# Retention and a Strassen-like MoE on one core: loads, GpSimd's share, w2's operands and the last additions put in another order

## The chip, the cores and the metric

The kernel runs on one core of a Trainium2 chip. The core has a matrix engine (TensorE, PE in the profile; its weight loads are PEld), three engines for elementwise work (VectorE is DVE, ScalarE is ACT, GpSimd is POOL) and a queue engine (SyncE, SP) that here issues nearly all DMAs. Each engine works through its own instructions in order and waits for others by semaphores, so an instruction that waits holds up all that stand behind it on the same engine. The metric is the device time of one execution in microseconds; a time is the median of several runs.

## The reference

Two stages follow each other. The first is a retention (a linear attention with decay) over 4 batches, 8 heads, 768 positions and 64 values per head:

```python
for t in range(S):
    state = gamma * state + k[t] (outer) v[t]
    y[t] = scale * q[t] @ state
```

Its output, seen as x of 3072 tokens with 512 values, goes through four experts, every token through all of them, weighted by normalised probabilities p:

```python
for e in range(4):
    h = np.maximum(x @ w1[e], 0.0)            # 512 -> 1024
    out += p[:, e:e + 1] * (h @ w2[e])        # 1024 -> 512
```

Inputs and outputs are float32.

## The kernel before, in words

**Precision.** A float32 product is made of three matmuls of the faster float32r kind: each operand is split into a high part (a copy by ACT, called hi, L237, L278, L287, L446) and a low part (source minus high part, on DVE or POOL, called lo, L241, L283, L291, L451), and hi·hi, hi·lo and lo·hi are added up in PSUM.

**Retention** works in chunks of 128 positions, six per batch. For chunk ci: scale_v multiplies v by the decay inside the chunk (POOL), scores multiplies keys with queries (PE) and masks the result (DVE, L143, tile sp), values multiplies the masked scores with v and the queries with the old state (PE, L181 and L187) and scales the result into xraw (DVE, L196); state makes the chunk's own k·v (PE, L154), added to the old state (DVE, L160), which decay has multiplied before (POOL, L166). values(ci - 1) also issues the matmuls of state(ci).

**The MoE** is cut into rounds: 16 per batch (NRND), each with 256 of the hidden units of one expert, so 64 rounds n in all. In each round x @ w1 is done as a 2x2 block product with 7 instead of 8 multiplications (p1, steps k = 0 to 6 in the order SEQ; i names the product, `p1(n, i)` has six matmuls of 384 columns). It needs sums of blocks of x (combine_x: t1, t2, t4 and one in place) and of w1 (combine_w1), and the products are put together by DVE additions in PSUM (L424) and ACT copies (L418). PSUM has two banks for the running product x, one for y, one for z, two for outputs. The first addition of a round's first result is called c11.

**Batch 0 and the others differ.** In batch 0, while w1 and w2 of a round come from memory for the first time, the hidden values get ReLU (ACT, L438) and low part (DVE, L439), and `p2(n - 1, tile)` multiplies 128 tokens of the round before with w2 (six matmuls of 512 columns); DVE adds the result, weighted with pm, to acc (L549). Beside it, weights(n, k), called once per step, splits w1 of round n + 1 and w2 of round n and writes all split operands to memory (save_w1, save_w2): w2's plain parts (hi2 and lo2 with wt2) and its combined ones (combine_w2, in place, then hi2 and lo2 with wc2). Later batches fetch them from there (fetch_w1 four steps ahead, fetch_w2). In these batches (n >= 16) the second product also has 7 multiplications and runs over pairs of rounds q: unit(q, s) with s = 0 to 13 is product UNITS[s] for one half d of the output. Its operands come from gated: ReLU times gate on DVE (L458), differences on POOL (L460), op_hi and op_lo. A unit's result is added to sums in SBUF (L582 for sum with sum, L424 for PSUM with sum), and the last pair of a batch leads to finish, which joins the sums and stores them. The units of the very last pair run after all rounds, alone: the tail.

**Order.** The whole program is written out by hand (`tc.manual_schedule()`); the framework places only semaphores and buffers. Within a step the order is: fetches, pass_step (runs what was put in the list soon with a delay in steps), p1, unit or p2, low parts of x of the next batch (in round 15 of a batch), weights, and a part of the next batch's retention (att_steps). A buffer is given again when its last reader is done: raw w1 has two, raw w2 one, plain w2 operands two, combined ones one, fetched w1 five. Batch 0's chunk loads borrow buffers of weights not yet in use.

Of the kernel before, what the change touches and what calls it, by code (L numbers as in the profile page):

```python
# [22 lines left out]
XPOOL = (1, 3)  # L23
WARM = (384, 384, 384, 384)
# [19 lines left out]
LAST_UNITS = tuple((i, d) for i in (1, 3, 5, 7, 6, 4, 2) for d in range(2))  # L44
# [7 lines left out]
def retention_moe(ctx: ExitStack, tc: tile.TileContext, qk, kv, w1, w2, probs, probt, cmask, cqs, cks, cys, out, out_t):  # L52
# [67 lines left out]
    def load_kv(ci, pool=None, tag=None, eng=None):  # L120
        if ci < NCH:
            t = (pool or in_p).tile([128, 2, H, D], F32, tag=tag or "kv", name="kv", bufs=None if pool else 2)
            (eng or nc.sync).dma_start(out=t, in_=kv[ci])
            raw_kv[ci] = t
# [186 lines left out]
    def units(q):  # L311
        return LAST_UNITS if q == NP * B - 1 else UNITS

# [8 lines left out]
    def fetch_w2(g):  # L322
        q, k = divmod(g, 7)
        if q < NP * B:
            i = units(q)[2 * k][0]
# [3 lines left out]
    def first_x(c, part):  # L329
        o = slice(C * c, C * c + C)  # L330
        combine_x(0, c, nc.vector, nc.gpsimd, part)
        for i in (7, 3, 4) if part else (5, 6):
            x_hi(0, i, o)
            x_lo(0, i, o)

    def weights(n, k):

        m = n + 1
        if n == 0:
            if k == 0:  # L340
# [107 lines left out]
    def op_lo(n, i):  # L448
        hi, lo, t = op[n, i]
        eng = nc.gpsimd if i in LO_POOL else nc.vector  # L450
        eng.tensor_tensor(out=lo, in0=t, in1=hi.bitcast(F32), op=ALU.subtract)  # L451

    def gated(n, key, src):

        f, j = key
        t = npool["b"].tile([128, HB], F32, tag="b", name="b")
# [4 lines left out]
        if key in ((0, 0), (1, 1)):  # L461
            i = 1 if key == (0, 0) else 3
            soon.append((0, lambda: op_hi(n, i, t)))
            soon.append((1, lambda: op_lo(n, i)))
        elif key == (0, 1):
            b11, b22, b12 = hb[n, (0, 0)], hb[n, (1, 1)], t

            soon.append((1, lambda: (sub(b11, b12, b11), sub(b12, b22, b12), sub(b22, b22, b11))))
            soon.append((2, lambda: op_hi(n, 5, b11)))
            soon.append((2, lambda: op_lo(n, 5)))  # L470
            soon.append((3, lambda: (op_hi(n, 7, b12), op_hi(n, 6, b22))))
            soon.append((3, lambda: (op_lo(n, 7), op_lo(n, 6))))
        else:
            b22 = hb[n, (1, 1)]
            soon.append((1, lambda: op_hi(n, 2, t)))
            soon.append((2, lambda: op_lo(n, 2)))
            soon.append((3, lambda: sub(t, t, b22)))
            soon.append((4, lambda: op_hi(n, 4, t)))
            soon.append((5, lambda: op_lo(n, 4)))
# [77 lines left out]
    def unit(q, k):  # L557
        i, d = units(q)[k]
# [18 lines left out]
    def finish(b, i, d):  # L577
# [255 lines left out]
```

## Time and profile before

| | |
|---|---|
| time, median of 3 runs | 1083.79 us (1083.56 to 1084.08) |
| the profiled execution | 1080.76 us |
| its span, first to last instruction | 1078.9 us |
| busy: PE, DVE, POOL, ACT | 1048.2, 731.2, 673.0, 378.7 us |
| granted TensorE clock, mean | 0.993 |
| moved by DMA | 293.70 MB, 272 GB/s over the span |
| the chain that ended last, by engine | PE 85%, DVE 8%, issue 3%, DMA 2% |

Rows of the profile's groups give engine, line, operation, the tiles written and read, shapes and count, then busy time in us and the mean duration of one in ns, then idle time of the engine before them and what ended it. Rows of a timeline give the start in us, the duration in us (of several merged instructions, from the first's start to the last's end), the engine and line, and in brackets the idle time before with the instruction that ended it. In the table by stage, each engine's busy time is followed by its number of instructions in parentheses. A matmul's duration is its latency; consecutive ones overlap.

### The profile page before, as it was taken

To read this page: it belongs to the slowest core of one execution; us is meant where nothing else is said; L and a number is where in the kernel's file an instruction comes from. 1 tells how busy PE (TensorE), PEld (TensorE's weight loads), DVE (VectorE), ACT (ScalarE), POOL (GpSimd) and SP (SyncE) were. 2 spreads that over 40 slices of the span, in tenths; PEclk is the share of its full clock that TensorE was granted. 3 is DMA by queue.
4 is the path that set the end of the run, shared out by engine and by line. 5 is a ranking of instruction groups with operands and counts; after the bars stand their busy time and mean duration, and the time that the engine had idled before them with its cause. 6 is when DMAs were issued, how large, how long until landed. Compare 5 with 4: busy or idle time off the path is not lost.

```text
span 1078.9 us, 18574 instructions
## 1 busy us (share of the span) xinstructions
PE 1048.2 (97%) x6696; PEld 991.3 (92%) x6696; DVE 731.2 (68%) x1221; ACT 378.7 (35%) x737; POOL 673.0 (62%) x638
## 2 busy tenths in 40 slices
PE   7789999999999999999999999999999999999997
PEld 5578888888888999999999999999999999999996
DVE  5957666666676476676679566677678746667667
ACT  2343433444443423222253433322234443333331
POOL 3577676767626556556479655656568865555566
PEclk9899999999999999999999999999999999999999
DMA  8479999899988788878788987888788988888875
GB/s 327 147 255 330 348 303 310 296 349 309 310 293 304 259 272 269 273 249 262 263 256 263 315 278 234 278 261 262 233 254 266 288 271 251 262 259 255 265 235 176
DMA packets 154603, 293.70 MB, mean 272 GB/s; under 512 B 12688, under 2 KB 77328, under 8 KB 154512
## 3 DMA queue, kind: packets, MB, share of 16 engines
q1 hardware_dynamic: 153792, 291.66, 83.0%
q8 instruction: 53, 0.87, 0.3%
q10 hardware_dynamic: 720, 0.86, 0.2%
q14 instruction: 38, 0.31, 0.1%
HBM read 223.22 MB, written 69.26 MB: 271 GB/s over the span
## 4 chain that ended last, share of the span: by engine, by line
PE 85%; DVE 8%; issue 3%; DMA 2%; POOL 1%; ACT 1%; ACTq 0%; SPq 0%; POOLq 0%; DVEq 0%
PE ps_u L567 31%; PE ps_x L506 23%; PE ps_z L506 11%; PE ps_o L541 10%; PE ps_y L506 5%; PE ps_s L140 2%; PE ps_v L187 2%; DVE xl L241 1%; DVE sum L582 1%; DMA w2r<-in_w 1%; PE ps_v L181 1%; DVE ol L451 1%; DMA w1r<-in_w 1%; DVE sum L424 1%; DMA ks<-in_cks 1%
## 5 line engine op out<-in xcount | busy, mean ns | idle before, releaser
L567 PE MATMUL ps_u<-oh,v 128*128 128x384 f32 x1344 | 395.2, 335 | 5.7 <-DVE sum L424 5.4
L460 POOL TENSOR_TENSOR b<-b 128x384 f32<-128x384 f32 x192 | 204.6, 1066 | 175.2 <-DVE b L458 145.4
L451 POOL TENSOR_TENSOR ol<-b,oh 128x384 fp32r<-128x384 f32 x192 | 211.2, 1112 | 81.8 <-ACT oh L446 44.6
L567 PEld LDWEIGHTS ps_u<-oh,v 128*128 128x128 f32 x1344 | 247.7, 188 | 8.7 <-DVE sum L424 7.3
L424 DVE TENSOR_TENSOR sum<-ps_u,sum 128x384 f32<-128x384 f32 x294 | 161.6, 550 | 134.2 <-PE ps_u L567 134.2
L446 ACT ACTIVATE oh<-b 128x384 fp32r<-128x384 f32 x336 | 163.5, 520 | 201.1 <-POOL b L460 109.0
L506 PE MATMUL ps_x<-xh,v 128*128 128x384 f32 x768 | 227.3, 337 | 0.7 <-ACT u L418 0.7
L567 PE MATMUL ps_u<-ol,v 128*128 128x384 f32 x672 | 224.9, 335 | 0.0
L418 ACT ACTIVATE u<-ps_x 128x384 f32<-128x384 f32 x128 | 62.7, 490 | 246.0 <-PE ps_x L506 245.9
L506 PEld LDWEIGHTS ps_x<-xh,v 128*128 128x128 f32 x768 | 141.4, 188 | 3.0 <-ACT u L418 1.0
L451 DVE TENSOR_TENSOR ol<-b,oh 128x384 fp32r<-128x384 f32 x144 | 130.3, 905 | 15.3 <-ACT oh L446 15.3
L506 PE MATMUL ps_x<-xl,v 128*128 128x384 f32 x384 | 128.4, 334 | 0.0
L567 PEld LDWEIGHTS ps_u<-ol,v 128*128 128x128 f32 x672 | 126.3, 188 | 0.0
L506 PE MATMUL ps_z<-xh,v 128*128 128x384 f32 x384 | 113.9, 337 | 2.2 <-DVE c2l L291 1.8
L549 DVE SCALAR_TENSOR_TENSOR acc<-ps_o,pm,acc 128x512 f32<-128x512 f32 x90 | 67.0, 744 | 51.9 <-PE ps_o L541 51.9
L541 PE MATMUL ps_o<-w2h,hh 128*128 128x512 f32 x192 | 75.5, 393 | 0.3 <-DVE acc L549 0.2
L541 PE MATMUL ps_o<-w2h,hl 128*128 128x512 f32 x192 | 75.8, 395 | 0.0
L541 PE MATMUL ps_o<-w2l,hh 128*128 128x512 f32 x192 | 75.8, 395 | 0.0
L506 PEld LDWEIGHTS ps_z<-xh,v 128*128 128x128 f32 x384 | 70.7, 188 | 3.7 <-DVE c2l L291 2.1
L506 PEld LDWEIGHTS ps_x<-xl,v 128*128 128x128 f32 x384 | 72.1, 188 | 0.1
L506 PE MATMUL ps_z<-xl,v 128*128 128x384 f32 x192 | 64.2, 334 | 0.0
L424 DVE TENSOR_TENSOR ps_y<-ps_y,u 128x384 f32<-128x384 f32 x64 | 36.0, 563 | 32.0 <-PE ps_y L506 32.0
(109 smaller groups left out, 1627.9 us busy)
## 6 DMA issues: line engine op xcount, KB each, us to landing
v<-k SPq DMA_DIRECT2D x336, 256.0 KB, 3.9
v<-k SPq DMA_DIRECT2D x168, 512.0 KB, 4.5
k<-w1h SPq DMA_DIRECT2D x16, 896.0 KB, 6.3
k<-w1l SPq DMA_DIRECT2D x16, 896.0 KB, 8.1
qk<-in_qk SPq DMA_DIRECT2D x24, 512.0 KB, 5.6
kv<-in_kv SPq DMA_DIRECT2D x23, 512.0 KB, 5.7
w1r<-in_w SPq DMA_DIRECT2D x16, 512.0 KB, 7.9
w2r<-in_w SPq DMA_DIRECT2D x16, 512.0 KB, 4.2
```

The source lines that it names most:

```text
L140: nc.tensor.matmul(ps[r][:, p, :], lhsT=a[rows, 1, p, :], rhs=a[rows, 0, p, :], start=True, stop=True)
L181: nc.tensor.matmul(ps[r][64 * k:64 * k + 64, half, :], lhsT=yst[(c - 1) % 2][rows, p, :], rhs=raw_qk[ci][rows, 0, p, :], start=(half == 0) ...
L187: nc.tensor.matmul(ps[r][64 * k:64 * k + 64, half, :], lhsT=v[:, 1, h, :], rhs=sp[:, h, :], start=(c == 0 and half == 0), stop=True, skip_ ...
L418: nc.scalar.activation(out=t, in_=ps, func=ACTF.Copy)
L424: nc.vector.tensor_tensor(out=o, in0=ps, in1=u, op=ALU.add)
L446: nc.scalar.activation(out=hi, in_=t, func=ACTF.Copy)
L451: eng.tensor_tensor(out=lo, in0=t, in1=hi.bitcast(F32), op=ALU.subtract)
L460: sub = lambda o, a, b: nc.gpsimd.tensor_tensor(out=o, in0=a, in1=b, op=ALU.subtract)
L506: nc.tensor.matmul(ps, lhsT=lhsT[:, cs], rhs=rhs[:, kt, :], start=(fresh and m == 0), stop=(m == 5), skip_group_check=True,)
L541: nc.tensor.matmul(ps, lhsT=a[:, ts], rhs=b[:, fs, :], start=(m == 0), stop=(m == 5))
L549: nc.vector.scalar_tensor_tensor(out=acc[nt], in0=ps, scalar=sc, in1=acc[nt], op0=ALU.mult, op1=ALU.add)
L567: nc.tensor.matmul(ps, lhsT=w[:, r, l, ds], rhs=o, start=(m == 0), stop=(m == 5))
```

## The change: what it does

Five things are put in another order or given to another engine.

1. *Loads and batch 0's retention.* mask and ks are loaded ahead of the first kv on ACT's queue; on SP's queue all twelve chunk loads and w1(0) come ahead of w2(0), w1(1) and the probabilities, and chunks 3 and 4 of kv go to the buffers of w2's combined operands. scale_v(ci + 1) is issued ahead of decay(ci + 1). Combining w1(0), its low parts, and the low parts of x parts 1 and 3 go from DVE to POOL; w2(0)'s low part and the probabilities' normalisation (first_gates) move into round 0; x parts 3, 4 and 7 are split whole and not chunk by chunk.
2. *Round 0.* w1(1)'s high parts move to steps 4 and 5, its low parts are both POOL's.
3. *w2's operands, rounds 1 to 15.* The plain parts of w2(n) are made in steps 4 and 5 (before: 1 and 2) and saved in step 6 with combine_w2 behind; the combined parts follow in steps 0 to 2 of the next round. load_w2(n) is issued in step 1 of round n (before: step 5 of round n - 1), save_w1 one step earlier.
4. *The change from batch 0 to batch 1.* The first four fetches of w1 are issued at the start of round 14; in round 15 POOL makes the low parts of five of the seven x parts (before: two); in round 16 the delays of gated are doubled. In all later rounds the operands 6 and 7 are made ahead of 5.
5. *The tail.* The last pair uses the same order of units as all others; 3 and 5 get the sums of others earlier, and unit 5 is added from PSUM to both 3 and 5; the halves of finish change engines, and the last low part of operand 5 goes to DVE.

```diff
+XPOOL0 = (0, 2, 4, 5, 6)
-LAST_UNITS = tuple((i, d) for i in (1, 3, 5, 7, 6, 4, 2) for d in range(2))
...
-    def first_x(c, part):
-        o = slice(C * c, C * c + C)
+    def first_part(c, part):
         combine_x(0, c, nc.vector, nc.gpsimd, part)
-        for i in (7, 3, 4) if part else (5, 6):
-            x_hi(0, i, o)
-            x_lo(0, i, o)
+        if part == 0:
+            o = slice(C * c, C * c + C)
+            for i in (5, 6):
+                x_hi(0, i, o)
+            for i in (5, 6):
+                x_lo(0, i, o)
     def weights(n, k):
         m = n + 1
         if n == 0:
             if k == 0:
-                first_x(2, 0)
-                first_x(1, 1)
-                first_x(2, 1)
+                x_hi(0, 3)
+                for c in range(3):
+                    first_part(c, 1)
+                x_hi(0, 7)
+                x_lo(0, 7)
+                x_hi(0, 4)
+                x_lo(0, 3, eng=nc.gpsimd)
+                x_lo(0, 4)
                 combine_w1(1, nc.gpsimd)
+                first_gates()
             elif k == 3:
                 kept.pop("c11")()
+            elif k == 4:
                 w1_hi(1, 0)
-                w1_lo(1, 0, nc.vector)
-                load_w1(2)
+                w1_lo(1, 0, nc.gpsimd)
+                lo2(0, wt2, nc.vector)
+            elif k == 5:
                 w1_hi(1, 1)
                 w1_lo(1, 1, nc.gpsimd)
-            elif k == 4:
-                save_w2(0, wt2, 0)
-                combine_w2(0, nc.gpsimd)
-            elif k == 5:
-                hi2(0, wc2, "c2")
                 save_w1(0)
             elif k == 6:
-                lo2(0, wc2, nc.vector)
-                load_w2(1)
-                save_w1(1)
+                combine_w2(0, nc.gpsimd)
+                save_w2(0, wt2, 0)
             return
         if k == 0:
-            save_w2(n - 1, wc2, 4)
+            if n == 1:
+                save_w1(1)
+            hi2(n - 1, wc2, "c2")
             if m < NRND:
                 load_w1(m + 1)
                 combine_w1(m, nc.gpsimd)
                 w1_hi(m, 0)
         elif k == 1:
-            hi2(n, wt2, "w2")
+            lo2(n - 1, wc2, nc.vector)
+            load_w2(n)
             if m < NRND:
                 w1_lo(m, 0, nc.gpsimd)
         elif k == 2:
-            lo2(n, wt2, nc.vector)
+            save_w2(n - 1, wc2, 4)
             if n == 2:
                 gates()
-        elif k == 3:
-            save_w2(n, wt2, 0)
-            combine_w2(n, nc.gpsimd)
-            if m < NRND:
-                w1_hi(m, 1)
+        elif k == 3 and m < NRND:
+            w1_hi(m, 1)
         elif k == 4:
-            hi2(n, wc2, "c2")
-        elif k == 5:
+            hi2(n, wt2, "w2")
             if m < NRND:
                 w1_lo(m, 1, nc.gpsimd)
-            lo2(n, wc2, nc.vector)
-            load_w2(n + 1)
-        elif k == 6 and m < NRND:
-            save_w1(m)
+        elif k == 5:
+            lo2(n, wt2, nc.vector)
+            if m < NRND:
+                save_w1(m)
+        elif k == 6:
+            combine_w2(n, nc.gpsimd)
+            save_w2(n, wt2, 0)
...
     def op_lo(n, i):
-        eng = nc.gpsimd if i in LO_POOL else nc.vector
+        eng = nc.gpsimd if i in LO_POOL and not (i == 5 and n == NRND * B - 1) else nc.vector
...
     def gated(n, key, src):
+        slow = 2 if n == NRND else 1
+        later = lambda w, what: soon.append((w * slow, what))
...
-            soon.append((2, lambda: op_hi(n, 5, b11)))
-            soon.append((2, lambda: op_lo(n, 5)))
-            soon.append((3, lambda: (op_hi(n, 7, b12), op_hi(n, 6, b22))))
-            soon.append((3, lambda: (op_lo(n, 7), op_lo(n, 6))))
+            later(2, lambda: (op_hi(n, 6, b22), op_lo(n, 6)))
+            later(2, lambda: (op_hi(n, 7, b12), op_lo(n, 7)))
+            later(3, lambda: (op_hi(n, 5, b11), op_lo(n, 5)))
...
     def unit(q, k):
+        elif q == NP * B - 1 and i == 5:
+            for o in (3, 5):
+                add(ps, psum[b, o, d], psum[b, o, d])
         else:
             add(ps, psum[b, i, d], psum[b, i, d])
...
     def finish(b, i, d):
         if b == B - 1:
-            e = (pool, dve)[d]
+            e = (dve, pool)[d]
             if i == 1:
                 sums(1, e, 2, 1)
-            elif i == 5:
-                sums(1, e, 3, 5)
             elif i == 6:
                 sums(0, e, 6, 1)
+                sums(1, e, 3, 6)
+                sums(1, e, 3, 5)
+            elif i == 7:
                 sums(0, e, 7, 6)
-                sums(0, e, 3, 6)
+                sums(0, e, 5, 7)
+                sums(1, e, 4, 7)
+            elif i == 5:
                 store(0, 3, 0, 1)
-                sums(0, e, 5, 7)
                 store(0, 5, 1, 1)
             elif i == 4:
-                sums(0, e, 4, 7)
                 store(0, 4, 1, 0)
...
+        nc.scalar.dma_start(out=mask, in_=cmask)
+        nc.scalar.dma_start(out=ks, in_=cks)
         load_qk(0)
         load_kv(0, eng=nc.scalar)
...
+        load_w1(0)
         load_qk(3, w_p, "w1l")
-        load_w1(0)
+        load_kv(3, v_p, "c2h", 1)
+        load_qk(4)
+        load_kv(4, v_p, "c2l", 1)
+        load_qk(5, v_p, "w2h")
+        load_kv(5, v_p, "w2l")
+        load_w2(0)
+        load_w1(1)
         nc.sync.dma_start(out=pr, in_=probs)
         nc.sync.dma_start(out=gr, in_=probt)
...
+        scale_v(0)
         for ci in range(NCHB):
             old = ci > 0
-            scale_v(ci)
             scores(ci)
             if ci == 5:
-                first_x(0, 1)
+                first_part(0, 0)
...
             if ci + 1 < NCHB:
+                scale_v(ci + 1)
                 decay(ci + 1)
             if ci == 1:
                 w1_hi(0, 0)
-                combine_w1(0, nc.vector)
-                w1_lo(0, 0, nc.vector)
+                combine_w1(0, nc.gpsimd)
             elif ci == 2:
                 w1_hi(0, 1)
-                w1_lo(0, 1, nc.vector)
...
+                w1_lo(0, 0, nc.gpsimd)
             elif ci == 3:
-                hi2(0, wt2, "w2")
-                lo2(0, wt2, nc.vector)
                 for i in (1, 2):
                     x_hi(0, i)
-                    x_lo(0, i)
             elif ci == 4:
-                first_x(0, 0)
+                w1_lo(0, 1, nc.gpsimd)
+                x_lo(0, 1, eng=nc.gpsimd)
+                x_lo(0, 2)
+                hi2(0, wt2, "w2")
+                load_w1(2)
...
-            elif ci == 5:
-                first_x(1, 0)
         start[0] = False
+        first_part(1, 0)
         values(ci, False)
+        first_part(2, 0)
...
-                fetch_w1(t + 4)
+                if t == 7 * (NRND - 2):
+                    for x in range(4):
+                        fetch_w1(7 * NRND + x)
+                if t >= 7 * NRND:
+                    fetch_w1(t + 4)
...
-                    e = nc.gpsimd if k in XPOOL else nc.vector
+                    e = nc.gpsimd if k in (XPOOL if g else XPOOL0) else nc.vector
...
-                if n == NRND and k == 0:
+                elif n == NRND and k == 0:
+                    hi2(n - 1, wc2, "c2")
+                elif n == NRND and k == 1:
+                    lo2(n - 1, wc2, nc.vector)
                     save_w2(n - 1, wc2, 4)
```

More of the change, by code (lines that the diff above doesn't have):

```diff
@@ L118, in load_qk, with load_kv @@
             raw_qk[ci] = t
-    def load_kv(ci, pool=None, tag=None, eng=None):
+    def load_kv(ci, pool=None, tag=None, bufs=None, eng=None):
         if ci < NCH:
-            t = (pool or in_p).tile([128, 2, H, D], F32, tag=tag or "kv", name="kv", bufs=None if pool else 2)
+            t = (pool or in_p).tile([128, 2, H, D], F32, tag=tag or "kv", name="kv", bufs=bufs if pool else 2)
             (eng or nc.sync).dma_start(out=t, in_=kv[ci])
@@ L309, in retention_moe @@
     wp1, wp2 = {}, {}
-    def units(q):
-        return LAST_UNITS if q == NP * B - 1 else UNITS
     def fetch_w1(g):
@@ L324, in fetch_w2 @@
         if q < NP * B:
-            i = units(q)[2 * k][0]
+            i = UNITS[2 * k][0]
             wp2[q, i] = npool["v2"].tile([128, 2, 2, 256], F32R, tag="v2", name="v2")
             nc.sync.dma_start(out=wp2[q, i].bitcast(F32), in_=kept2[q % NP][:, A2_AT[i]])
-    def first_x(c, part):
-        o = slice(C * c, C * c + C)
+    def first_part(c, part):
         combine_x(0, c, nc.vector, nc.gpsimd, part)
-        for i in (7, 3, 4) if part else (5, 6):
-            x_hi(0, i, o)
-            x_lo(0, i, o)
+        if part == 0:
[4 more added lines that the diff above has]
+                x_lo(0, i, o)
     def weights(n, k):
@@ L462, in gated @@
             i = 1 if key == (0, 0) else 3
-            soon.append((0, lambda: op_hi(n, i, t)))
-            soon.append((1, lambda: op_lo(n, i)))
+            later(0, lambda: op_hi(n, i, t))
+            later(1, lambda: op_lo(n, i))
         elif key == (0, 1):
             b11, b22, b12 = hb[n, (0, 0)], hb[n, (1, 1)], t
-            soon.append((1, lambda: (sub(b11, b12, b11), sub(b12, b22, b12), sub(b22, b22, b11))))
-            soon.append((2, lambda: op_hi(n, 5, b11)))
-            soon.append((2, lambda: op_lo(n, 5)))
-            soon.append((3, lambda: (op_hi(n, 7, b12), op_hi(n, 6, b22))))
-            soon.append((3, lambda: (op_lo(n, 7), op_lo(n, 6))))
+            later(1, lambda: (sub(b11, b12, b11), sub(b12, b22, b12), sub(b22, b22, b11)))
+            later(2, lambda: (op_hi(n, 6, b22), op_lo(n, 6)))
+            later(2, lambda: (op_hi(n, 7, b12), op_lo(n, 7)))
+            later(3, lambda: (op_hi(n, 5, b11), op_lo(n, 5)))
         else:
             b22 = hb[n, (1, 1)]
[L475 to L479, printed above, removed]
+            later(1, lambda: op_hi(n, 2, t))
+            later(2, lambda: op_lo(n, 2))
+            later(3, lambda: sub(t, t, b22))
+            later(4, lambda: op_hi(n, 4, t))
+            later(5, lambda: op_lo(n, 4))
     def pass_step():
@@ L557, in unit @@
     def unit(q, k):
-        i, d = units(q)[k]
+        i, d = UNITS[k]
         b, qb = divmod(q, NP)
@@ L654, in retention_moe @@
         nc.vector.memset(warm, 0.0)
+        nc.scalar.dma_start(out=mask, in_=cmask)
+        nc.scalar.dma_start(out=ks, in_=cks)
         load_qk(0)
         load_kv(0, eng=nc.scalar)
-        nc.scalar.dma_start(out=ks, in_=cks)
-        nc.scalar.dma_start(out=mask, in_=cmask)
+        nc.scalar.dma_start(out=ys, in_=cys)
         nc.scalar.dma_start(out=qs, in_=cqs)
@@ L661, in retention_moe @@
         load_kv(1)
-        nc.scalar.dma_start(out=ys, in_=cys)
         load_qk(2, v_p, "w2l")
         load_kv(2, w_p, "w1h")
+        load_w1(0)
         load_qk(3, w_p, "w1l")
-        load_w1(0)
+        load_kv(3, v_p, "c2h", 1)
[5 more added lines that the diff above has]
+        load_w1(1)
         nc.sync.dma_start(out=pr, in_=probs)
         nc.sync.dma_start(out=gr, in_=probt)
-        load_w2(0)
-        load_qk(4)
-        load_kv(3)
-        load_qk(5, v_p, "w2h")
-        load_kv(5, v_p, "w2l")
-        load_kv(4)
-        load_w1(1)
         wps = ps_z.tile([128, 512], F32, tag="z", name="ps_w")
```

9 lines of the change are left out of this document (5 added, 4 removed).

## The prediction

> **What bounds the kernel now.** I read the page's engine shares first, then a table of busy time by stage, then what TensorE (PE) waited for, and last the timelines of the stages in which it waited.
>
> ```profile
> PE 1048.2 (97%) x6696; PEld 991.3 (92%) x6696; DVE 731.2 (68%) x1221; ACT 378.7 (35%) x737; POOL 673.0 (62%) x638
> ```
> ```profile
> 0.00:25.00 25.00, 17.70 (x224) 13.09 (x226) 14.11 (x29) 4.38 (x5) 7.12 (x11) 0.95 0.94 352
> 25.00:50.00 25.00, 18.71 (x176) 15.34 (x174) 24.12 (x40) 10.07 (x23) 13.76 (x14) 0.85 0.49 159
> 50.00:75.00 25.00, 20.19 (x108) 17.20 (x109) 14.32 (x23) 9.58 (x16) 19.42 (x18) 1.00 0.62 200
> 75.00:100.00 25.00, 24.93 (x137) 21.88 (x136) 16.58 (x27) 11.01 (x18) 15.71 (x16) 1.00 0.94 317
> ...
> 300.00:350.00 50.00, 46.88 (x251) 42.00 (x250) 33.19 (x51) 20.22 (x40) 23.66 (x22) 1.00 0.93 318
> ...
> 1060.00:1079.00 19.00, 12.22 (x60) 10.75 (x60) 12.14 (x18) 0.52 (x1) 11.11 (x10) 0.86 0.54 184
> ```
>
> PE is busy for 1048.2 of 1078.9 us. The columns of the table are the stretch, its length, then busy time of PE, its weight loads, VectorE (DVE), ScalarE (ACT) and GpSimd (POOL), the granted clock, the DMA share and GB/s. The 30.7 us that are missing lie in few places: 18.4 in the first 75 us (7.3, 6.3 and 4.8), 3.1 at 300 to 350, 6.8 after 1060. From 75 us on PE has 24.93 of 25. Only these three places can give anything, and the long middle can only lose. In the first, DVE is the limit: 24.12 of 25 at 25 to 50 us, with PE at a clock of 0.85 besides.
>
> ```profile
> 6.08 1.16 PE L140 MATMUL ps_s<-qk 64*128 64x128 f32 x16
> ...
> 17.00 1.16 PE L140 MATMUL ps_s<-qk 64*128 64x128 f32 x16
> ...
> 23.12 1.12 PE L154 MATMUL ps_v<-kv 128*64 128x64 f32 x16 [2.72 <-POOL kv L128]
> 24.17 2.08 PE L140 MATMUL ps_s<-qk 64*128 64x128 f32 x16
> ...
> 37.97 0.69 PE L506 MATMUL ps_x<-xh,w1h 128*128 128x384 f32 x1
> ...
> 54.70 0.39 PE L541 MATMUL ps_o<-w2h,hh 128*128 128x512 f32 x1
> ...
> 57.76 0.45 PE L506 MATMUL ps_x<-xh,w1h 128*128 128x384 f32 x1 [1.51 <-ACT u L418]
> ...
> 65.02 0.44 PE L506 MATMUL ps_x<-xh,w1h 128*128 128x384 f32 x1 [2.11 <-ACT u L418]
> ```
>
> Retention of batch 0 ends at 37.97, where round 0's first matmul starts. One wait for scaled values (2.72) is followed by scores that take 2.08 instead of 1.16: PE at half clock. The first token matmul (p2) comes at 54.70; after it two waits for ACT remain, 1.51 and 2.11.
>
> **The change, part by part. 1: retention of batch 0.**
>
> ```profile
> L241 DVE TENSOR_TENSOR xl<-t,xh 128x256 fp32r<-128x256 f32 x9 | 7.3, 840 | 0.0
> L143 DVE TENSOR_TENSOR sp<-ps_s,mask 128x512 f32<-128x512 f32 x8 | 5.1, 677 | 0.0
> L196 DVE TENSOR_TENSOR xr<-ps_v,qs 128x256 f32<-128x256 f32 x11 | 4.1, 411 | 0.0
> ...
> L241 DVE TENSOR_TENSOR xl<-xr,xh 128x768 fp32r<-128x768 f32 x2 | 3.1, 1578 | 0.0
> ...
> L160 DVE TENSOR_TENSOR yst<-ps_v,yst 128x256 f32<-128x256 f32 x4 | 1.6, 411 | 0.0
> L213 DVE TENSOR_TENSOR t<-xr,t 128x256 f32<-128x256 f32 x3 | 1.6, 524 | 0.1
> L213 DVE TENSOR_TENSOR t<-xr 128x256 f32<-128x256 f32 x3 | 1.2, 407 | 0.0
> ...
> L291 DVE TENSOR_TENSOR w2l<-w2r,w2h 128x1024 fp32r<-128x1024 f32 x1 | 1.2, 1212 | 0.0
> ```
> ```profile
> 50.34 2.39 POOL L283 TENSOR_TENSOR w1l<-s,w1h 128x1024 fp32r<-128x1024 f32 x1 [3.71 <-ACT w1h L278]
> 52.68 0.74 POOL L296 TENSOR_TENSOR w2r<-w2r 128x256 f32<-128x256 f32 x1
> ...
> 59.81 1.84 POOL L283 TENSOR_TENSOR w1l<-w1r,w1h 128x768 fp32r<-128x768 f32 x1
> ```
>
> These are the groups of DVE between 14 and 50 us, and POOL's prices. w1's combination (4 operations), both its low parts and two x low parts of round 0 go to POOL: 4 x 0.74 + 2.39 + 3 x 1.84 = 10.9 us there. w2's low part (1.2) and the gates go behind; x's parts 3, 4 and 7 become whole operations (128x768), nine of 128x256 become two on DVE and one on POOL. By 14.4 us DVE has done chunk 1's state, which I leave where it is. From there to the first addition of round 0 (c11) it keeps masks 5.1; values 10 x 0.37 = 3.7; states 3 x 0.4 = 1.2; combinations of x 1.6 + 1.2 = 2.8; six low parts of a chunk 6 x 0.84 = 5.0; three whole ones 3 x 1.58 = 4.7; the gates about 1.6 (an estimate: four small operations at the 0.4 of the nearest rows). That is 24.1, so c11 at 38.5, and with about 1 us in which DVE waits for PE, 39.5.
>
> PE allows it: scores came at 6.08 and, three chunks on, at 17.00, so 3.64 a chunk with the waits for scaled values in it. With scale_v ahead of decay on POOL, and mask and ks ahead of the first kv, six chunks end at 28 us at the latest. The loads allow it too: 352 GB/s over the first 25 us brings the twelve chunk loads and w1 (6.8 MB) in by some 20 us. Their order costs nothing while a pair (1 MB, 3.0 us) lands in less than a chunk takes; without that cover each late pair costs its delay once. load_w2(0), load_w1(1) and the probabilities move behind the chunks on SP's queue; POOL needs w1(1) and DVE the probabilities only past 30 us.
>
> ```profile
> 47.51 0.55 DVE L424 TENSOR_TENSOR ps_y<-ps_y,u 128x384 f32<-128x384 f32 x1
> ```
>
> c11 stood at 47.51, so 8.0 earlier. Both ends: without any contention (0.42 for 128x256, 0.95 for 128x768) DVE keeps some 18 to 19 us, but part 7's combinations on POOL then hold c11 at about 36.5; if every two-input operation of DVE and every one of POOL exclude each other, the list after 22 us (DVE 7.9, POOL 13.5) ends at 43.4.
>
> The Trainium skill speaks against this part (SBUF — State Buffer, Who interferes with whom): a DVE instruction with two SBUF inputs and a GpSimd instruction that reads SBUF exclude each other for the whole instruction. By that rule this step would gain 4.1 and not 8.0. The groups above show the effect (840 ns for what takes 410 alone), but the tail's rows below show less than full exclusion.
>
> **2: rounds 0 and 1.** After c11 everything is a chain, because w1_hi(1,·) now stand behind the ReLUs of steps 4 and 5 on ACT, lo2(0) stands ahead of the addition of step 5 on DVE, and both w1_lo(1,·) are POOL's: c11 and its parts 1.7, the next addition with ReLU and low part 1.5, lo2 1.2 (+0.6 against POOL), addition and ReLU 1.0, w1_hi about 1.0, w1_lo 2.39, the rest of p1(1,5) 0.9, dispatch 0.5: 10.8. The first p2 comes at 50.3 instead of 54.70: of the 8.0, 4.4 survive.
>
> ```profile
> 63.53 1.06 ACT L287 ACTIVATE w2h<-w2r 128x1024 fp32r<-128x1024 f32 x1 [4.71 <-DMA w2r<-in_w]
> ```
> ```profile
> 75.98 1.39 PE ps_o L541 x6
> 77.37 1.04 PE ps_x L506 x6
> ```
>
> Then the waits of 1.51 and 2.11 go. The second arose because ACT stood 4.71 behind w2(1)'s load; hi2(1) now comes at step 4. The first came from hi2(0,c2) behind POOL's combine_w2. That wait stays on ACT, half a round later: with w1_lo(1,1) done at T, combine_w2(0) ends at T + 3.0, hi2 T + 4.1, w1_hi(2,0) T + 4.9, two copies T + 5.9; PE asks for the second at T + 7.2 (two p1 at 1.04, three p2 at 1.39 and the 0.9). Hidden by 1.3 us. So 4.4 + 3.6 = **8.0** for parts 1 and 2, between 4 and 11.
>
> **3: rounds 1 to 15.** Same operations, same bytes, other places.
>
> ```profile
> w1r<-in_w SPq DMA_DIRECT2D x16, 512.0 KB, 7.9
> w2r<-in_w SPq DMA_DIRECT2D x16, 512.0 KB, 4.2
> ```
>
> load_w2(n) moves from step 5 of the round before to step 1, past save_w1 (2 DMAs), save_w2 of the plain half (2) and load_w1. So it meets the backlog that w1's load meets now: 7.9 us to landing, not 4.2. A round is 7 p1 and 6 p2, 15.6 us, and about 16.2 with scores and values of the next batch. Issued when lo2 of the combined half is done (1.04 + 1.04 + 1.2 = 3.3 us into the round), it lands at 11.2; hi2 stands at step 4 (9.4), behind it on ACT are the ReLUs of steps 5 and 6 and the first copy of the next round; p2 asks for w2's parts and these ReLUs at 18.3. hi2 and lo2 take 2.3, so 4.8 us are spare: nothing. POOL's three combinations and low parts per round keep their sum. I take **0**; a landing later than 12.7 us after issue would cost its excess in each of 15 rounds.
>
> **4: the change of batch (300 to 350).**
>
> ```profile
> 309.30 1.66 SPq L320 DMA_DIRECT2D v<-k  x1
> ```
> ```profile
> 316.26 0.41 PE L506 MATMUL ps_z<-xh,v 128*128 128x384 f32 x1 [1.78 <-DVE c2l L291]
> ```
>
> PE waits 1.78 for its second operand of round 16. The wait is put down to c2l, which that matmul does not read; its operand's fetch was issued at 309.30 behind saves. I take the fetch for the cause. Either way it goes: the first four fetches come two rounds earlier, and c2l a step later with x's low parts moved from DVE (three of 0.95) to POOL, which has no w1 work in round 15. hi2(15,c2) can hold ACT for some 3.4 us of round 16, under the six p2 of steps 1 to 3. I take **-2.0** with 0.2 of a smaller wait; ends 0 and -2.7.
>
> **5: the tail.**
>
> ```profile
> L582 POOL TENSOR_TENSOR sum<-sum 128x384 f32<-128x384 f32 x7 | 8.2, 1189 | 1.6 <-DVE sum L424 1.5
> ...
> L582 DVE TENSOR_TENSOR sum<-sum 128x384 f32<-128x384 f32 x7 | 7.2, 1047 | 0.1
> ```
> ```profile
> 1057.40 0.53 ACT L446 ACTIVATE oh<-b 128x384 fp32r<-128x384 f32 x1 [0.56 <-POOL b L460]
> ```
> ```profile
> 1072.34 0.44 PE L567 MATMUL ps_u<-oh,v 128*128 128x384 f32 x1 [3.14 <-DVE sum L424]
> ```
> ```profile
> 1058.81 0.56 DVE L424 TENSOR_TENSOR sum<-ps_u,sum 128x384 f32<-128x384 f32 x1
> ...
> 1075.47 0.56 DVE L424 TENSOR_TENSOR sum<-ps_u,sum 128x384 f32<-128x384 f32 x1 [1.14 <-PE ps_u L567]
> ```
>
> The 3.14 us wait goes: four sums in a row on DVE held the accumulators. But the count of sums stays 7 on each engine, two PSUM additions (0.56 each) and lo5 come to DVE, and 6 and 7 now come before 5. hi6 waits for POOL's third difference until 1057.40, and hi7, hi2, hi5 stand behind it at some 0.5 each. DVE holds at lo5, ahead of the addition of unit 3,0, until hi5 (1059.3) and POOL's lo6 and lo7 (1060.1, at 1.1 each, an estimate between 0.74 for 256 elements and 1.84 for 768). lo2 and one sum follow, so that addition runs at about 1061.5 and not 1058.8, and PE, with two accumulators, starts unit 6,0 2.1 us late. After it, sums at 1.05 beside POOL hold PE by 1 to 1.6 us at units 5 and 4, and the last addition ends at 1076.7 against 1076.0; with sums at 0.56 PE sets the pace and it ends at 1073.6. Ends +0.7 and -2.4; I take **-0.8**.
>
> **The sum**: -8.0 - 2.0 - 0.8 = -10.8. The profiled run took 1080.76, so 1070.0; the median of the runs is 3.03 above it, so 1083.79 - 10.8 = **1073.0**. Best ends: -11 - 2.7 - 2.4 = -16.1, 1067.7. Worst: -4 + 0 + 0.7 = -3.3, 1080.5.
>
> **Rivals.** *Contention eats the start*: c11 at 43.4, the upper end of part 1, gives 4.1 less in parts 1 and 2; with the rest as forecast -6.9, 1076.9. For it: POOL's load between 22 and 43 us doubles. Against it: seven pairs of sums took 8.2 and 7.2 us, about 1.2 a pair, where exclusion would need 0.56 and some 1.0 (POOL's estimate above) one after the other. It is what the section of the Trainium skill named in part 1 would make of this change. *Everything free*: DVE and the tail at their uncontended prices, -16, 1067.8. *Nothing gained*: a chunk's load or the chain of part 2 takes the place of DVE and the first p2 stays at 54.7; the two ACT waits (3.6) are moved and not removed; only parts 4 and 5 are left: -2.8, 1081.0. Against it: the groups show 10 us of work leaving DVE. *Slower*: w2 lands late in every round, because save_w1, save_w2 and load_w1 are ahead of it on SP's queue at a DMA share of 0.94. It decides beyond 12.7 us from issue to landing; one us past it costs 15, so -10.8 + 15 = +4, 1088. Against it: w1's load, in the same place now, takes 7.9.
>
> **Chances**: forecast 0.50, contention 0.20, free 0.12, nothing 0.08, slower 0.10. A difference of 0.2% (2.2 us) is about what can be told from none. Faster takes the first three and the edge of the fourth, 0.83; same the rest of the fourth, whose time lies at that mark, 0.07; slower 0.10. The range holds the first three with the bounds above: 1067 to 1080.
>
> **What would show it.** Part 1: the first matmul of round 0 near 27 to 29 us, scores at 1.16 throughout, c11 at 36 to 43. Part 2: first p2 at about 50, and no ACT wait of over 1 us behind it. Part 3: PE at 24.9 of 25 from 75 to 300 us, w2's landing under 12 us. Part 4: no wait of 1.8 us at the second operand of round 16. Part 5: no wait of 3 us, a wait of about 2 at unit 6,0. It is wrong if PE has gaps that recur every 16 us, or if the first p2 stays at 54.

## The result and the profile after

The changed kernel takes 1078.18 us (median of 4 runs, 1077.64 to 1078.53) where the kernel before takes 1083.86 (4 runs, 1083.56 to 1084.08): ratio 0.9947, 95% interval 0.993 to 0.9965. It is 5.7 us faster. The forecast was 10.8 faster, 1073.0; the measured time lies inside the range of 1067 to 1080, 5.2 above the forecast itself.

The page's engine shares and the table of busy time by stage, changed kernel (columns as in the prediction):

```profile
PE 1050.2 (98%) x6696; PEld 993.5 (92%) x6696; DVE 732.7 (68%) x1206; ACT 378.6 (35%) x731; POOL 682.0 (63%) x649
```
```profile
0.00:25.00 25.00, 21.27 (x264) 16.94 (x264) 10.48 (x21) 5.20 (x6) 11.58 (x17) 0.86 0.87 332
25.00:50.00 25.00, 17.24 (x143) 13.62 (x139) 22.07 (x33) 8.20 (x16) 18.56 (x18) 0.80 0.46 158
50.00:75.00 25.00, 22.53 (x112) 19.49 (x112) 14.30 (x21) 10.38 (x17) 20.86 (x19) 0.86 0.90 292
75.00:300.00 225.00, 225.00 (x1362) 198.74 (x1361) 156.52 (x234) 92.07 (x146) 155.67 (x146) 1.00 0.95 320
300.00:350.00 50.00, 49.05 (x275) 44.00 (x275) 35.24 (x51) 21.96 (x44) 28.73 (x25) 1.00 0.84 286
```

PE is busy for 2.17 us more in 300 to 350 (46.88 before) and has no gap at all from 75 to 300. In the first 75 us it is busy for 61.0 instead of 56.6, but look at the clock: 0.86, 0.80, 0.86, where it was 0.95, 0.85, 1.00. Part of the time gained is matmuls that take longer.

The timeline of PE, then of DVE and POOL, in the start of the changed kernel:

```profile
6.44 1.16 PE L140 MATMUL ps_s<-qk 64*128 64x128 f32 x16
10.02 1.12 PE L154 MATMUL ps_y<-kv 128*64 128x64 f32 x16 [2.42 <-POOL kv L128]
11.07 2.08 PE L140 MATMUL ps_s<-qk 64*128 64x128 f32 x16
...
30.10 0.44 PE L517 MATMUL ps_x<-xh,w1h 128*128 128x384 f32 x1
...
52.63 0.69 PE L517 MATMUL ps_x<-xh,w1l 128*128 128x384 f32 x1 [2.03 <-POOL w1l L283]
...
56.80 0.62 PE L552 MATMUL ps_o<-w2h,hh 128*128 128x512 f32 x1
...
68.25 1.16 PE L140 MATMUL ps_s<-qk 64*128 64x128 f32 x16
```
```profile
28.95 1.95 DVE L213 TENSOR_TENSOR t<-xr 128x256 f32<-128x256 f32 x1
30.93 1.91 DVE L213 TENSOR_TENSOR t<-xr,t 128x256 f32<-128x256 f32 x1
...
35.18 0.41 DVE L213 TENSOR_TENSOR t<-xr 128x256 f32<-128x256 f32 x1
...
46.32 0.55 DVE L434 TENSOR_TENSOR ps_y<-ps_y,u 128x384 f32<-128x384 f32 x1
```
```profile
28.27 2.35 POOL L283 TENSOR_TENSOR w1l<-s,w1h 128x1024 fp32r<-128x1024 f32 x1
30.58 1.98 POOL L241 TENSOR_TENSOR xl<-xr,xh 128x768 fp32r<-128x768 f32 x1
```

Retention now ends at 30.10 (37.97 before), 7.9 earlier. But the first addition of round 0 (c11) comes at 46.32, only 1.2 earlier, the first token matmul (p2) at 56.80, which is 2.1 later than before, and the next anchor in both kernels, the scores of chunk 7 (counted from one; the first of the next batch), at 68.25 instead of 70.09. Two combinations of DVE, 0.41 each when alone, take 1.95 and 1.91: each ends some 0.3 after the POOL operation beside it.

The DMA issues by size, and PE's waits in the tail:

```profile
w1r<-in_w SPq DMA_DIRECT2D x16, 512.0 KB, 6.7
w2r<-in_w SPq DMA_DIRECT2D x16, 512.0 KB, 4.3
```
```profile
1057.59 0.44 PE L578 MATMUL ps_u<-oh,v 128*128 128x384 f32 x1 [2.06 <-DVE sum L434]
1063.15 0.45 PE L578 MATMUL ps_u<-oh,v 128*128 128x384 f32 x1 [0.90 <-DVE sum L434]
1065.70 0.44 PE L578 MATMUL ps_u<-oh,v 128*128 128x384 f32 x1 [1.24 <-DVE sum L434]
1068.74 0.45 PE L578 MATMUL ps_u<-oh,v 128*128 128x384 f32 x1 [0.31 <-DVE sum L434]
```

w2's load lands after 4.3 us in its new place. In the tail one wait of 3.14 has become four, 4.5 together.

### The profile page after: what moved, and what is told of

The parts are those of the page before. It is cut to its first block, busy times and chain, and to the rows that moved or that the text cites. A ratio compares the mean times of both kernels' runs of the same rounds, so it can differ in the third digit from the quotient of the medians.

```text
span 1076.6 us, 18570 instructions
## 1 busy us (share of the span) xinstructions
PE 1050.2 (98%) x6696; PEld 993.5 (92%) x6696; DVE 732.7 (68%) x1206; ACT 378.6 (35%) x731; POOL 682.0 (63%) x649
## 4 chain that ended last, share of the span: by engine, by line
PE 88%; DVE 7%; POOL 1%; ACT 1%; DMA 1%; issue 1%; POOLq 0%; ACTq 0%; DVEq 0%
PE ps_u L578 30%; PE ps_x L517 23%; PE ps_z L517 12%; PE ps_o L552 11%; PE ps_y L517 6%; PE ps_s L140 2%; PE ps_v L187 2%; DVE sum L596 1%; PE ps_v L181 1%; DVE sum L434 1%; DVE ol L461 1%; DVE xl L241 1%; PE ps_v L154 1%; DMA kv<-in_kv 1%; DVE b L470 0%
## 5 line engine op out<-in xcount | busy, mean ns | idle before, releaser
L461 POOL TENSOR_TENSOR ol<-b,oh 128x384 fp32r<-128x384 f32 x191 | 199.9, 1065 | 63.7 <-ACT oh L456 57.6
L461 DVE TENSOR_TENSOR ol<-b,oh 128x384 fp32r<-128x384 f32 x145 | 135.1, 932 | 24.0 <-ACT oh L456 24.0
```

## The experiments

All times below are medians of their own runs, ratios are against the kernel before on the same chip; start times of the four anchors are from each profiled execution: the first matmul of round 0, where retention ends; c11; the first token matmul (p2); and the scores of chunk 7.

| kernel | retention ends | c11 | first p2 | chunk 7 | median | ratio, 95% interval |
|---|---|---|---|---|---|---|
| before | 37.97 | 47.51 | 54.70 | 70.09 | | |
| changed | 30.10 | 46.32 | 56.80 | 68.25 | 1078.18 | 0.9947, 0.993 to 0.9965 |
| before, again | 37.12 | 47.56 | 54.76 | 70.15 | 1084.32 | 1.0006, 0.9992 to 1.002 |
| changed, again | 27.32 | 43.52 | 53.99 | 66.41 | 1077.89 | 0.9943, 0.993 to 0.9956 |
| start as before | 38.75 | 47.84 | 55.03 | 66.25 | 1076.65 | 0.993, 0.9917 to 0.9942 |
| kv first | 26.81 | 43.03 | 53.33 | 64.53 | 1076.54 | 0.9936, 0.9917 to 0.9956 |
| w1(0) in part on DVE | 30.78 | 43.29 | 53.77 | 66.31 | 1078.47 | 0.9953, 0.9934 to 0.9971 |
| w1(1) in step 0 | 29.04 | 46.29 | 57.65 | 68.87 | 1079.38 | 0.9953, 0.9941 to 0.9966 |
| w1(1) in steps 0 and 4 | 28.82 | 45.02 | 52.68 | 63.88 | 1074.79 | 0.9923, 0.9905 to 0.994 |
| joined | 26.77 | 41.53 | 49.67 | 62.46 | 1070.86 | 0.9882, 0.9866 to 0.9898 |

**The spread: both kernels once more.** No edit.

> The kernel before, unchanged, for its spread. The changed kernel's median is 5.7 us lower, but its profiled execution only 2.4 us (1078.38 against 1080.76), because the profiled execution of before lies 3 us below all its timed ones. Theory A: that one execution was a lucky one and the span of before is usually 1081.5 to 1082.5, so a further profile shows waits in the first 75 us that the first one did not have. Rival B: a profiled execution of this program is always some 3 us shorter than a timed one; then the profiled run here is again near 1080.8 and the timed ones near 1083.8.

> The changed kernel once more, beside the others. Theory A (the start of the kernel varies with the clock that PE gets in its first 25 us, and the profile of the changed kernel fell on a slow start): another execution shows the retention's end at 27 to 28 instead of 30.10, the first addition of round 0 near 43.5, chunk 7 at 66.3; over its runs the time spreads from 1075 to 1080 with the median near 1077.5. Rival (the loads' new order makes that start slow every time): retention again ends near 30 and chunk 7 starts near 68.3.

The kernel before ran from 1080.02 to 1086.64 over all its runs; its profiled execution of 1080.76 was one of its quickest. So the two profiled executions differ by only 2.4 (1080.76 and 1078.38), the medians by 5.7. The new profile of the kernel before has a span of 1081.2 instead of 1078.9, but not where Theory A looked for the difference: its c11, first p2 and chunk 7 stand within 0.1 of the first profile's. Some 1.6 of the 2.3 come at the change of batch, where the same matmul waits in both (1.95 here, 1.78 there) and only here the matmuls behind it run at half clock (the next wait for ACT ends at 338.32 here, at 336.75 there):

```profile
316.27 0.41 PE L506 MATMUL ps_z<-xh,v 128*128 128x384 f32 x1 [1.95 <-DMA v<-k]
...
317.75 0.63 PE L541 MATMUL ps_o<-w2h,hh 128*128 128x512 f32 x1
```

The changed kernel's new profile, same code, in its start:

```profile
10.48 1.16 PE L140 MATMUL ps_s<-qk 64*128 64x128 f32 x16
...
27.32 0.44 PE L517 MATMUL ps_x<-xh,w1h 128*128 128x384 f32 x1
...
53.99 0.63 PE L552 MATMUL ps_o<-w2h,hh 128*128 128x512 f32 x1
```
```profile
16.35 0.76 DVE L196 TENSOR_TENSOR xr<-ps_v,qs 128x256 f32<-128x256 f32 x2 [0.81 <-PE ps_v L154]
...
19.74 0.75 DVE L196 TENSOR_TENSOR xr<-ps_v,qs 128x256 f32<-128x256 f32 x2 [1.02 <-PE ps_v L154]
...
23.10 0.76 DVE L196 TENSOR_TENSOR xr<-ps_v,qs 128x256 f32<-128x256 f32 x2 [1.00 <-PE ps_v L154]
...
38.80 1.97 DVE L241 TENSOR_TENSOR xl<-xr,xh 128x768 fp32r<-128x768 f32 x1 [0.58 <-ACT xh L237]
...
43.52 0.55 DVE L434 TENSOR_TENSOR ps_y<-ps_y,u 128x384 f32<-128x384 f32 x1
```

The second chunk's scores take 1.16 here and 2.08 above; the wait ahead of them is much the same (2.61 and 2.42). From there everything up to c11 is 2.8 earlier. So PE's clock alone moves the changed start by 2.8, from execution to execution; the loads' order does not make it slow every time.

**Is the reordered retention worth anything? The start as before.** Loads, retention and round 0 as in the kernel before; w2 half a round on, the change of batch and the tail as changed. Against the changed kernel:

```
-                w1_lo(1, 0, nc.gpsimd)
-                lo2(0, wt2, nc.vector)
+                w1_lo(1, 0, nc.vector)
...
-        load_w2(0)
+        load_kv(4)
...
-                scale_v(ci + 1)
...
-                combine_w1(0, nc.gpsimd)
+                combine_w1(0, nc.vector)
+                w1_lo(0, 0, nc.vector)
```

> The changed kernel with the loads, the retention of batch 0 and the order of round 0 as before; from round 1 on w2's operands are half a round on, and the change of batch and the tail are the changed ones. Theory A (the reordered retention is worth nothing or little, and what is gained by 75 us comes from the two waits for ACT that go): retention ends near 38, the first token matmul stands at 54.7, the waits of 1.51 and 2.11 after it are gone, so the scores of the next batch's chunk 7 start near 66.5 and the kernel takes 1076.5 to 1079, no slower than the changed one. Theory B (the reordered retention has its worth, and the waits for ACT went because of it): the chain after the first token matmul keeps a wait of 1 us or more, chunk 7 starts at 68.3 or later, and the time is 1079.5 to 1082.

Theory A holds: chunk 7 at 66.25, and 1076.65, no slower than the 1077.89 of the changed kernel on the same chip. The table of busy time for 50 to 60 us, first of the changed kernel (again), then of this one:

```profile
50.00:60.00 10.00, 9.57 (x34) 8.22 (x35) 3.55 (x4) 3.59 (x7) 9.47 (x10) 0.67 0.80 256
```
```profile
50.00:60.00 10.00, 8.50 (x43) 7.65 (x44) 6.08 (x9) 5.00 (x9) 8.93 (x9) 1.00 0.83 239
```

This is where the gain of the start goes, counted in the changed kernel's second profile. The new retention brings c11 forward by 4.3 (47.84 to 43.52). The new round 0 takes 10.5 from there to the first p2 instead of 7.2 and gives back 3.3. And from first p2 to chunk 7 the changed kernel takes 12.4 instead of 11.2: its PE is busier in those 10 us (9.57 against 8.50) and issues fewer matmuls (34 against 43), at a clock of 0.67. 4.3 - 3.3 - 1.2 leaves nothing. What both gain at chunk 7, 3.7 to 3.9 against the kernel before (1.8 in the changed kernel's first profile), is the two waits for ACT, which were 1.51 and 2.11; they are gone without the new start, with the shift of w2.

**Contention: w1's combination and first low part of round 0 on DVE, POOL's two long low parts one and two chunks earlier.**

```
-                combine_w1(0, nc.gpsimd)
+                combine_w1(0, nc.vector)
+                w1_lo(0, 0, nc.vector)
             elif ci == 2:
                 w1_hi(0, 1)
-                w1_lo(0, 0, nc.gpsimd)
+                w1_lo(0, 1, nc.gpsimd)
             elif ci == 3:
                 for i in (1, 2):
                     x_hi(0, i)
+                x_lo(0, 1, eng=nc.gpsimd)
             elif ci == 4:
-                w1_lo(0, 1, nc.gpsimd)
-                x_lo(0, 1, eng=nc.gpsimd)
```

> The changed kernel with w1(0)'s combination and first low part back on DVE, and with POOL's two long low parts (2.4 and 2.0 us) issued one chunk earlier, so that POOL is free when DVE makes the combinations and low parts of x. Theory A (exclusion of two-input DVE operations and POOL operations took the gain of the start: DVE's first two combinations took 1.95 and 1.91 instead of 0.41): they take 0.4 to 0.9, c11 comes at 42 to 44 and not 46.3, first p2 at 53 and not 56.8, 3 to 4 us faster than the changed kernel. Rival B (it is the work put on DVE that counts, wherever POOL is): DVE carries 2.7 us more, c11 no earlier than 46, time the same or up to 2 slower.

```profile
28.75 0.63 DVE L213 TENSOR_TENSOR t<-xr 128x256 f32<-128x256 f32 x1
29.42 0.42 DVE L213 TENSOR_TENSOR t<-xr,t 128x256 f32<-128x256 f32 x1
...
43.29 0.55 DVE L434 TENSOR_TENSOR ps_y<-ps_y,u 128x384 f32<-128x384 f32 x1
```

The mechanism is shown (1.95 and 1.91 become 0.63 and 0.42), and no time is won: DVE now has w1's work itself, retention ends 3.5 later than in the changed kernel's second profile (both at a clock of 1.00 in the first 25 us), and c11 comes at 43.29 instead of 43.52. The 3 to 4 us that Theory A hoped for were counted from c11 at 46.3, of which 2.8 was the clock. Work that POOL does while it shuts DVE out, and work that DVE does itself, cost the path the same here.

**The loads: the first kv ahead of ks and mask on ACT's queue.**

```
-        nc.scalar.dma_start(out=mask, in_=cmask)
-        nc.scalar.dma_start(out=ks, in_=cks)
         load_qk(0)
         load_kv(0, eng=nc.scalar)
+        nc.scalar.dma_start(out=ks, in_=cks)
+        nc.scalar.dma_start(out=mask, in_=cmask)
```

> The changed kernel with only the first four DMAs of ACT's queue in the order of before (kv, ks, mask). In the changed trace kv lands at 8.8 us and not 6.2, the first state matmuls wait 2.42 and PE runs at half clock until 16 us. Theory A (the late first kv costs): first state at 8.9 and not 10.0, no half clock, end of retention at 27.5 to 28.5 and not 30.1, and as DVE's list behind it starts with the last masks, c11 earlier by the same: 1.5 to 2.5 us faster than the changed kernel. Rival B (DVE and POOL set c11 whatever PE does): end of retention earlier, c11 at 46, time unchanged within 0.5.

The first wait for scaled values falls from 2.61 to 1.82, c11 is 0.5 earlier and chunk 7 1.9 earlier than in the changed kernel's better execution, 1.2 of it because the token matmuls keep their full clock (0.39). In the medians that is a ratio of 0.9936 against 0.9943 to 0.9947, which these runs can't tell apart.

**The chain of part 2: w1's parts of round 1 earlier.** First three of the four in step 0, and the second low part in step 4:

```
                 x_hi(0, 4)
+                w1_hi(1, 0)
                 x_lo(0, 3, eng=nc.gpsimd)
                 x_lo(0, 4)
+                w1_lo(1, 0, nc.gpsimd)
                 combine_w1(1, nc.gpsimd)
+                w1_hi(1, 1)
```

> The changed kernel with w1's high and low parts of round 1 issued in step 0 of round 0 (ACT and POOL) instead of behind the ReLUs of steps 4 and 5. Theory A (the 10.5 us from the first addition of round 0 to the first token matmul are the chain through w1's parts of round 1: ReLU, high part, low part of 2.4 to 2.6 on POOL): PE's waits of 2.03 and 0.44 for w1l go, the first token matmul follows 7 to 8 us after that addition, the time falls by 2 to 3. Rival (DVE's additions and ReLU low parts set that stretch, or the parts only crowd the end of the retention): the stretch stays above 9.5 us or the first addition comes later by as much, the time stays within 1.

Neither theory holds: the waits for w1l are gone, but a new one is longer. ACT's timeline, then PE's:

```profile
47.85 1.06 ACT L278 ACTIVATE w1h<-s 128x1024 fp32r<-128x1024 f32 x1 [5.90 <-POOL s L269]
48.81 0.47 ACT L428 ACTIVATE u<-ps_z 128x384 f32<-128x384 f32 x1
```
```profile
49.72 0.69 PE L517 MATMUL ps_x<-xh,w1h 128*128 128x384 f32 x1 [7.29 <-ACT u L428]
```

The second high part waits 5.90 on ACT for POOL's combination, and the copies of PE's products queue behind it. So the edit was repeated with that part, and its low part, in step 4, and the first low part behind the combination:

> The changed kernel with w1's first high and low part of round 1 in step 0 of round 0 (the low part behind the combinations on POOL) and its second ones in step 4, so that no high part on ACT waits for a combination ahead of the copies of x's products, as it did for 5.90 with all of them in step 0. Theory A (the chain through w1's parts sets the stretch from the first addition of round 0 to the first token matmul): PE's waits of 2.03 and 0.44 for w1l are gone or below 0.5 together, PE keeps its full clock there, the stretch is 7.5 to 8.5 instead of 10.5 and the time falls by 2 to 3. Rival (additions and ReLU low parts on DVE, one after the other, set it): the stretch stays above 9.5 and the time within 1 of the changed kernel.

```profile
45.02 0.55 DVE L434 TENSOR_TENSOR ps_y<-ps_y,u 128x384 f32<-128x384 f32 x1
```
```profile
51.25 0.44 PE L517 MATMUL ps_z<-xh,w1h 128*128 128x384 f32 x1 [1.44 <-DVE hl L449]
...
52.68 0.39 PE L552 MATMUL ps_o<-w2h,hh 128*128 128x512 f32 x1
```

Theory A holds: c11 to first p2 is 7.7 instead of 10.5, the token matmul takes 0.39 and not 0.62, and chunk 7 comes at 63.88, 2.5 before the changed kernel's second profile. The ratio falls to 0.9923, some 2.4 us better than the changed kernel's, but the intervals overlap; four of the six runs are below all ten of the changed kernel, two are not. What is left in that stretch is a wait of 1.44 for DVE.

**The change of batch: the four early fetches alone, in the kernel before.**

```
-                fetch_w1(t + 4)
+                if t == 7 * (NRND - 2):
+                    for x in range(4):
+                        fetch_w1(7 * NRND + x)
+                if t >= 7 * NRND:
+                    fetch_w1(t + 4)
```

> The kernel before with one edit: the first four fetches of kept w1 operands for the second batch are issued two rounds earlier. Theory A (the wait of 1.78 at 316 us is for such a fetch): the waits of PE between 300 and 350 us fall from 3.1 to about 1.2, the time by 1.8. Rival (it is for c2l, the low part on DVE that the trace names): the wait stays, the time is the same within 0.5.

1082.53 (12 runs, 1079.64 to 1083.68), ratio 0.9986, interval 0.9975 to 0.9997. PE's waits by cause from 300 to 350 us, in the kernel before (again), then here:

```profile
PE ps_z L506 <- DMA v<-k: 1.9, 1, 1.9
PE ps_x L506 <- ACT u L418: 1.1, 1, 1.1
```
```profile
PE ps_o L541 <- DVE acc L549: 1.3, 2, 1.1
PE ps_x L506 <- ACT u L418: 1.0, 1, 1.0
```

In the second profile of the kernel before the trace itself names the fetch, and with the early fetches that wait is gone: the fetch was the cause. But 1.3 of waits for p2's evictions on DVE come in its place, so that PE gains 0.6 in this stretch (47.48 busy against 46.88 and 46.91) and not 1.8. The changed kernel gains 2.17 there in its first profile, but over the nine profiles that have its change of batch PE is busy for 47.23 to 49.05, 1.3 more than before in the mean; waits of 0.5 to 0.9 for later fetches come back in some of them. What the other moves add, x's low parts off DVE above all, was not tried alone.

**The tail as before, everything else changed.**

```
-        elif q == NP * B - 1 and i == 5:
-            for o in (3, 5):
-                add(ps, psum[b, o, d], psum[b, o, d])
...
-            e = (dve, pool)[d]
+            e = (pool, dve)[d]
```

> The changed kernel with the tail of before (order of units, sums, engine halves, operands of the last round). My prediction gave the new tail a gain of 0.8; the two traces give it a loss: from the last p1 to the last addition 22.7 us against 22.1, and 1.0 more from the last addition to the end. Theory A (DVE's sums and the late low part of operand 5 hold PE; the new tail loses): 0.6 to 1.6 us faster than the changed kernel, about 1077. Rival B (the difference of the two ends is the chance of one execution): within 0.4 us of the changed kernel. Rival C (the new tail gains, as predicted): 0.8 slower, 1079.

```profile
1066.64 0.58 PE L588 MATMUL ps_u<-oh,v 128*128 128x384 f32 x1 [3.25 <-DVE sum L438]
```

The one wait is back, and from the start of the last p1 matmul to the start of the last addition it takes 21.5 (1049.05 to 1070.59). Over all profiles the old tail takes 21.2 to 21.9 (five executions, 21.5 in the middle), the new one 22.1 to 23.4 (seven, 22.2 in the middle). The two longest of these, 23.0 and 23.4, are those in which PE's clock fell in 1040 to 1060 (0.92 and 0.91). So the new tail costs about 0.7. The medians can't show it: 1077.42, a ratio of 0.9947, with the old tail, 0.9943 and 0.9947 with the new.

**All together:** kv first, w1(1) in steps 0 and 4, the tail as before, and the gates behind step 6:

```
                 combine_w2(0, nc.gpsimd)
                 save_w2(0, wt2, 0)
+                first_gates()
```

> The changed kernel with four edits at once: the first kv ahead of mask and ks, w1's parts of round 1 earlier, the gates of the first batch (1.45 on DVE just ahead of the first addition of round 0) behind step 6, and the tail as before. Theory A (the start is a chain through DVE and POOL up to the first token matmul, each step of it worth its own length): first addition at 41.6 (43.0 less 1.4), first token matmul at 49 to 50, chunk 7 of the next batch at 61 to 62, the time 1072 to 1075. Rival (PE's clock after its waits, or the loads, take it back): chunk 7 at 64 or later, the time 1076 or more.

```profile
41.53 0.55 DVE L438 TENSOR_TENSOR ps_y<-ps_y,u 128x384 f32<-128x384 f32 x1
```
```profile
48.23 0.44 PE L527 MATMUL ps_z<-xh,w1h 128*128 128x384 f32 x1 [1.69 <-DVE hl L453]
...
49.67 0.61 PE L562 MATMUL ps_o<-w2h,hh 128*128 128x512 f32 x1
...
62.46 1.16 PE L141 MATMUL ps_s<-qk 64*128 64x128 f32 x16
```

c11 and the first p2 come where they were expected, chunk 7 is 0.5 late because the first six token matmuls run at half clock (0.61 to 0.63). At 1070.86 us (4 runs, 1070.52 to 1073.31) this kernel is quicker than expected (1072 to 1075) and beats both: 13.1 under the kernel before, some 7 under the changed one. One wait of 1.69 is left in its start: w2's low part on DVE stands ahead of the addition and the low parts that PE waits for. With the start as before, chunk 7 came at 66.25; so the new start, once mended in this way, is worth 3.8 there.

## Why the prediction was right and wrong

The side was right, and so were most mechanisms; the size was not, because of part 1. The time lies in the range because the range was drawn to hold the contention rival too: the forecast was 10.8, and 5.7 came.

**Part 1 failed.** c11 was put at 39.5 and came at 46.32, or at 43.52 in the execution whose retention ran at full clock. Two terms of its sum were too small. DVE's short operations beside POOL were priced at their mean, 2.8 for the six combinations. The first pair met POOL's two long low parts and took 3.9, and all six took 5.5. And 1 us was allowed in which DVE waits, where 3.4 came (the four rows with brackets in the second profile). That is 2.7 and 2.4 too little, of which about 1 comes back because DVE's rows overlap: the 4.0 from 39.5 to 43.5. The upper bound, 43.4 under full exclusion, is close to what came. The rule of the Trainium skill (SBUF — State Buffer, Who interferes with whom), a lock held for the whole instruction, agrees with the rows above, where 0.41 becomes 1.95 beside 2.35. That the bound fits to 0.1 is in part chance, for its list has no waits in it. The rows of the tail's sums, which were held against it, are means over all seven; in the kernel before, the four that DVE and POOL do side by side end after 5.4 us (1066.43 to 1071.82), where one after the other would need some 6.2 (0.55 and 1.01 each when alone). So they do hold each other up there too, though not quite for their whole lengths.

The other 2.8 is PE's clock, which the sum did not have. With mask and ks ahead of it the first kv lands late. In the six profiles with that order PE waits 1.76 to 2.92 for the first scaled values, and in three of them it falls to half clock around that wait.

**Part 2** had the length right, 10.8 forecast and 10.5 measured, and the two ACT waits went as it said. Its 4.4 that survive the chain rested on c11 at 39.5. With c11 at 43.5, 0.7 survived at the first p2 (54.70 to 53.99), and half clock after it took that away. The start as before, without the reordered retention, gains the same 3.9 at chunk 7. So parts 1 and 2 gave 1.8 in the first profile, 3.7 in the second, instead of 8.0, and all of it is the part put at 3.6 for the ACT waits. The rival *Contention eats the start* described it best: c11 at 43.4 takes 3.9 from the 8.0 and leaves 4.1 for parts 1 and 2. (The prediction calls the 4.1 the loss; its -6.9 and 1076.9 are rightly worked out with 3.9.)

**Part 3** was right: no gap from 75 to 300 us. w2's landing was forecast at 7.9 and took 4.3; the slower rival had no ground.

**Part 4** was right on the cause: the fetch was what the named wait was for. Its -2.0 is about right, but it varies from execution to execution. From the scores of chunk 7 to the last p1 matmul the kernel before takes 984.2 and 985.8 in its two profiles, and the nine with the new change of batch take 981.7 to 983.8, 982.7 in the mean. That is 1.5 less than the first and 3.1 less than the second, which lost 1.6 to the clock. The early fetches alone gave 1.3 by the medians.

**Part 5** had the wrong sign: about +0.7 instead of -0.8. The path was right (the wait of 2.1 at unit 6,0 is there, 2.06, and waits of 0.9 and 1.2 follow), but the value was taken between its two ends, and the contended end, +0.7, is what came.

**The offset**: the profiled execution of before was rightly read as a quick one; its clock held at the change of batch. By stages, the first pair of profiles differs by -1.8 at chunk 7, -2.4 from there to the last p1, +1.0 in the tail and +1.0 behind the last addition, together the 2.3 between their spans. The second pair differs by -3.7, -4.1, +1.2 and nothing, together 6.7. The 5.7 of the medians lies between them.

## What to carry to other kernels

A gain at one point of a start counts for what reaches the next point at which the engine that sets the end is saturated; try the parts alone before crediting any of them. A short VectorE operation with two SBUF inputs beside a long GpSimd one is to be priced by what is left of the long one, not by a mean; and taking an operation from one of the two to the other frees nothing while they exclude each other. Look in an engine's queue for what stands just ahead of the instruction that all wait for: here w1's parts of the next round, taken out of that stretch, brought chunk 7 forward by 2.5 us, and the whole reordering of the retention was worth nothing until they were out of it.

## What the runs showed of the hardware

PE's clock falls after waits that are short, and not every time. No wait of PE in the changed kernel between 30 and 57 us is over 2.1 us, yet its first token matmul takes 0.62 instead of 0.39, and in its second profile the clock of 50 to 60 us is 0.67. After a wait of 1.44, the kernel with w1(1) in steps 0 and 4 kept its full clock (0.39), after 1.69 the joined kernel lost it (0.61). The same start ran at 0.86 in its first 25 us in one execution and at 1.00 in another, after much the same wait. Nor is it the longer wait that costs the clock: of the six profiles with mask and ks ahead of the first kv, those with waits of 1.76, 2.06 and 2.42 lost it, those with 2.61, 2.67 and 2.92 did not. What goes with the loss here is a later start: the first scores stand at 6.44 to 6.74 in the three that lost it, after matmuls that took longer from the beginning, and at 6.02 to 6.10 in the others. The Trainium skill (TensorE: Matmul & The Clock Gate, Part 1) has a free-running window of some 3.4 us and a fall to half rate after an idle one. That a window's phase decides agrees with the two executions; that a whole window must be idle does not fit here, where 1.69 to 2.42 were enough. This case did not show what share of a window has to be idle.
